# Transfers recorded by modelled readiness on their queue, and the softmax reciprocals broadcast by four short transfers a unit

## The chip, the cores and the metric

One core of one Trainium2 chip. The metric is the device time of one execution in microseconds (us). "Before" is the kernel without the change, "after" the kernel with it.

## The reference

Two layers of attention and a gated feed-forward block, batch 1, 2048 tokens, width 512, 32 heads of 16, feed-forward width 1792, bfloat16 inputs:

```python
x = A_x
for _ in range(2):
    n = layernorm(x)
    q, k, v = heads_of(n @ wqkv)                    # 32 heads of 16
    x = x + (softmax(q @ k.T / 4) @ v) @ wo
    n = layernorm(x)
    x = x + (gelu(n @ w_gate) * (n @ w_up)) @ w_down
```

## The kernel before

The kernel's Python code is itself a scheduler. It keeps a modelled clock for each engine, always picks what can start next, and *records* it. What is recorded is a fixed order of instructions on each engine, with semaphore waits between them. If an engine's next instruction is not ready, the engine stands: in the profile below TensorE stood 16.8 us in all before matmuls whose input had not landed. So the numbers that the scheduler *books* for an instruction or a transfer decide the order, and the chip then executes that order with the durations that the trace shows.

A transfer is booked as 0.5 us of its queue, `kb / 180` us of a shared wire, and 1.7 us to land:

```python
def dma(eng, grp, dst, src, r=(), w=(), serial=False, kb=32):
    ...
    t = max(sch.free[eng], sch.ready(eng, r, w)) + 0.5
    wire[0] = max(t, wire[0]) + kb / 180.0
    return sch.op(eng, lambda e: e.dma_start(dst, src), r=r, w=w, grp=grp, cost=0.5, lat=wire[0] - t + 1.7)
```

A *unit* is four heads for 512 query tokens. After its scores, exponentials and products with V, the unnormalised output lies in `OS` (128 partitions: 32 for each head, of which 16 hold the output, one the sum). A query block has eight units. For each half of them the sums are gathered into `LT`, inverted by VectorE, stored to a scratch tensor in HBM, and broadcast back to the partitions of `OS`; GpSimd (POOL) multiplies. Odd units land in `ATS` and are moved into the other half of `AT` by four small transfers. Then TensorE can do the output projection (`AT` times `WO`), and the feed-forward of this query block runs between the attention of the next ones:

```python
def normalise(layer, qb, gs, half):
    ...                                              # checks, reciprocal of LT on VectorE
    def then(o):
        dma("sp", "rs%d" % half, RSC[half, 0:np_, :], LT[0:np_, :], r=lk, w=[("RSC", half)], serial=True)
        rest = list(enumerate(gs))
        def spread():
            ...                                      # next unit, one of NRB = 2 buffers
            dma("sp", "rb%d" % slot, RB[:, slot, :],
                AP(RSC, (half * 16 * HB + 16 * i) * 128, [[512, 4], [0, 32], [1, 512]]),
                r=[("RSC", half)], w=[("RB", slot)], serial=True, kb=256)
            ...
            def done(o):
                if odd:
                    for j in range(4):
                        dma("sp", "at%d_%d" % (c % 2, j), AT[32 * j + 16:32 * j + 32, c, :],
                            ATS[32 * j:32 * j + 16, c % 2, :], r=[("ATS", c % 2)], w=[("ATo", c, j)], serial=True)
                ...
                spread()
            job("pool", 1, [(lambda e: e.tensor_tensor(dst, OS[:, os_, :], RB[:, slot, :], op=ALU.mult), ...)], done)
        for _ in range(NRB):
            spread()
    dve(1, ops, then)
```

Every transfer that SyncE (SP) issues is recorded at the moment at which the code comes upon it, even if it will only be ready some us later; what is recorded after it on that queue waits behind it. The feed-forward weights come on the same queue, in chunks of 256 KB through six buffers:

```python
def wload():
    ...
    dma("sp", "wr%d" % s, dst, src, w=[("WR", s)], serial=True, kb=256)
```

and `w_down` is read once for each of a query block's four tiles, except at the end of the program, where four accumulators are held at once:

```python
wlist += [("d", i) for _ in range(1 if tail else 4) for i in range(NFT // 2)]
```

Of the kernel before, what the change touches and what calls it, by code (L numbers as in the profile page):

```python
# [11 lines left out]
ALU = mybir.AluOpType  # L12
# [163 lines left out]
def _emit_fast(nc, es, x_in, wqkv, wo, wg, wu, wd, out, n_rep=2):  # L176
# [179 lines left out]
    def late_init():  # L356
        sch.op("pool", lambda e: e.memset(AP(VP, 16, [[NKT * H * VW, 128], [VW, NKT * H]]), 1.0), w=[("VPONE",)])
        sch.op("pool", lambda e: e.memset(OKL[:], 1.0), w=[("OKL",)])
        sch.op("pool", lambda e: e.memset(OKV[:], 1.0), w=[("OKV",)])
        sch.op("pool", lambda e: e.memset(LT[:], 1.0), w=[("LT", i) for i in range(HB)])  # L360
# [6 lines left out]
    for layer in range(n_rep):  # L367
        for qb in range(NQB):
            tail = layer == n_rep - 1 and qb == NQB - 1
            wlist += [("g", i) for i in range(NFT // 2)] + [("u", i) for i in range(NFT // 2)]  # L370
            wlist += [("d", i) for _ in range(1 if tail else 4) for i in range(NFT // 2)]
    wst = {"loaded": 0, "next": 0}

    def wload():
        i = wst["loaded"]
        if i >= len(wlist):
            return
        wst["loaded"] += 1
        kind, k = wlist[i]
        s = i % NWR  # L380
        if kind == "d":
            dst = WR[:, s, 0:2 * D].rearrange("p (a b) -> p a b", a=2)
            src = wd_src[:, 2 * k:2 * k + 2, :]
        else:
            dst = WR[:, s, 0:NCK * 256].rearrange("p (a b) -> p a b", a=NCK)
            src = (wg_src if kind == "g" else wu_src)[:, :, 256 * k:256 * (k + 1)]
        dma("sp", "wr%d" % s, dst, src, w=[("WR", s)], serial=True, kb=256)

    def wget(kind, k):
        i = wst["next"]  # L390
        assert wlist[i] == (kind, k), (wlist[i], kind, k)
        wst["next"] += 1
        while wst["loaded"] < i + NWR:
            if wst["loaded"] >= len(wlist):
                break
            wload()
        return i % NWR


    jobs = {"dve": [], "pool": []}  # L400
    now = [0.0]
# [7 lines left out]
    def dve(prio, ops, then=None, ported=False):  # L409
        job("dve", prio, ops, then, ported)  # L410

    def starts_of(eng):
        out = []
# [5 lines left out]
    def pump_one(t):  # L419
        for eng in ("dve", "pool"):  # L420
            if not jobs[eng] or sch.free[eng] >= t:
# [143 lines left out]

    xloaded = set()

    def xset(n):
        return [4 * (n % 2) + i for i in range(4)]

    def xload(n):
# [6 lines left out]
        if layer:  # L578
            dma("sp", "xl%d" % (n % 2), X[:, sl[0]:sl[0] + 4, :], XS[rows, :].rearrange("(a p) c -> p a c", p=128),
                r=[("XS", 4 * qb + i) for i in range(4)], w=[("X", x) for x in sl], serial=True, kb=1024)  # L580
        else:
            def issue():
                return dma("pool", "xp%d" % (n % 2), X[:, sl[0]:sl[0] + 4, :],
                           x_in[0, rows, :].rearrange("(a p) c -> p a c", p=128),
                           w=[("X", x) for x in sl], serial=True, kb=1024)
            job("pool", 3, [(issue, [], [("X", x) for x in sl], None)])

# [112 lines left out]
    gq = []  # L700
    rb_no = [0]

    def normalise(layer, qb, gs, half):
# [12 lines left out]
        def then(o):  # L716
            dma("sp", "rs%d" % half, RSC[half, 0:np_, :], LT[0:np_, :], r=lk, w=[("RSC", half)], serial=True)
            rest = list(enumerate(gs))

            def spread():  # L720
                if not rest:
                    return
                i, g = rest.pop(0)
                slot = rb_no[0] % NRB
                rb_no[0] += 1
                dma("sp", "rb%d" % slot, RB[:, slot, :],
                    AP(RSC, (half * 16 * HB + 16 * i) * 128, [[512, 4], [0, 32], [1, 512]]),
                    r=[("RSC", half)], w=[("RB", slot)], serial=True, kb=256)
                os_ = os_of.pop((layer, qb * NG + g))
                c, odd = g // 2, g % 2  # L730
                dst = ATS[:, c % 2, :] if odd else AT[:, c, :]
                wk = [("ATS", c % 2)] if odd else [("AT", c)] + [("ATo", c, j) for j in range(4)]

                def done(o):
                    if odd:

                        for j in range(4):
                            dma("sp", "at%d_%d" % (c % 2, j), AT[32 * j + 16:32 * j + 32, c, :],
                                ATS[32 * j:32 * j + 16, c % 2, :], r=[("ATS", c % 2)], w=[("ATo", c, j)], serial=True)
                    os_free.append(os_)  # L740
                    done_n[0] += 1
                    if done_n[0] == n:
                        have.add(("norm", layer, qb, gs[-1]))
                    spread()
                job("pool", 1, [(lambda e: e.tensor_tensor(dst, OS[:, os_, :], RB[:, slot, :], op=ALU.mult),  # L745
                                 [("OS", os_), ("RB", slot)], wk, 1.35)], done)

            for _ in range(NRB):
                spread()
        dve(1, ops, then)  # L750

    def evac(layer, u, part):
# [11 lines left out]
        def then(o):  # L764
# [9 lines left out]
            while g >= lo + sizes[k]:  # L774
                lo += sizes[k]
                k += 1
            i = g - lo
            dma("sp", "lt%d" % i, LT[16 * i:16 * i + 16, :],
                AP(OS, 16 * NOS * 512 + s * 512, [[32 * NOS * 512, 4], [1, 512]]),
                r=[("OS", s)], w=[("LT", i)], serial=True)  # L780
            units_done[layer] += 1
            if i == sizes[k] - 1:
                normalise(layer, qb, list(range(lo, lo + sizes[k])), k % 2)
            if g == NG - 1:
# [25 lines left out]
    def post(layer, qb):  # L810
# [6 lines left out]
        xload(n_)  # L817
        while ("norm", layer, qb, NG - 1) not in have or n_ not in xloaded:
            yield None
# [18 lines left out]
        for k in range(NFT // 2):  # L838
            s = wget("u", k)
            for jj in range(2):  # L840
# [7 lines left out]
        for ts in ([tts] if tail else [[tt] for tt in tts]):  # L848
            bs = None
            for k in range(NFT // 2):  # L850
                s = wget("d", k)

# [15 lines left out]
            for tt, b in zip(ts, bs):  # L868
                i = tt % 4
                x = xsl[i]  # L870
                if last:
                    ob = XNT[:, i % NCK, 512 * qb + (i // NCK) * D:512 * qb + (i // NCK) * D + D]

                    def store(o, i=i, tt=tt, ob=ob):
                        dma("sp", "st%d" % i, out[0, tt * 128:(tt + 1) * 128, :], ob, r=[("OB", i)], serial=True)
                        have.add(("out", tt))
                    evac_job(1, b, [(lambda e, b=b, x=x, ob=ob: e.tensor_tensor(ob, bank(b)[:, 0:D], X[:, x, :],
# [5 lines left out]
                else:  # L883
                    def keep(o, i=i, tt=tt, x=x):
                        dma("sp", "xs%d" % i, XS[tt * 128:(tt + 1) * 128, :], X[:, x, :], r=[("X", x)],
                            w=[("XS", tt)], serial=True, kb=256)
                        stats(i, x, got(("st", (layer, qb, 1), i)))
                        if i == 3:
                            have.add(("xs", layer + 1, qb))
                    evac_job(1, b, [(lambda e, b=b, x=x: e.tensor_tensor(X[:, x, :], bank(b)[:, 0:D], X[:, x, :],  # L890
# [88 lines left out]
    def fill_ready():  # L979
# [6 lines left out]
        if gq:  # L986
            qb, k = gq[0]
            if wst["loaded"] <= wst["next"]:
                return None
# [22 lines left out]
    def g_slot(qb, k):  # L1012
        b0 = slot_banks()[0]
        take_slot()
        xs = slice(512 * qb, 512 * (qb + 1))
        s = wget("g", k)

# [184 lines left out]
    def head_source(b):  # L1202
# [6 lines left out]
        if b:  # L1209
            while b not in xloaded:  # L1210
                yield None
# [991 lines left out]
```

## Time and profile before

| | before |
|---|---|
| median, first three timed runs | 1823.64 us |
| span of the profiled run | 1823.5 us |
| ScalarE busy | 1530.2 us (84%) |
| TensorE busy | 1681.1 us, of which 271.8 are clock-keeping matmuls (zero weights; the scheduler inserts them in a function named `keep_clock`) |
| VectorE busy | 1410.7 us |

The page of the kernel before, its table of costliest groups (line, engine, operation, output and inputs, shapes, count, then busy us and mean ns, then the engine's idle time just before them and what ended most of it):

```profile
L1067 ACT ACTIVATE fPT<-fPS 128x1024 bf16<-128x1024 f32 (+1 forms) x1408 | 1449.9, 1175 | 177.1 <-PE fPS L1062 173.1
L1101 DVE TENSOR_SCALAR fPI<-fPS 128x512 int16<-128x512 f32 x956 | 631.0, 686 | 222.3 <-PE fPS L1062 218.5
...
L1192 PE MATMUL fPS<-fONB,fZV 128*17 128x512 bf16 x3496 | 271.8, 387 | 5.2 <-POOL fONB L344 4.1
```

ScalarE's exponentials (line 1067) set the pace: windows of 20 us without a disturbance show it busy for 20.00 of them. What there is to win is therefore its idle time, 293 us. I sorted every gap of ScalarE into kinds. *Head* is before 75 us, *tail* after the last exponential, *boundary* a gap of over 9 us in between (they lie between the layers), *GELU* a gap before a GELU. A gap is put down to the *projection* or the *weights* where TensorE, at that place or within 6 us before it, stood 0.4 us or more before a matmul that reads `fAT`, or a weight chunk. The rest is *other*.

TensorE's waits in the kernel before (engine, line, waited for: us in total, times, longest us):

```profile
PE fPS L1062 <- ACT fPT L1067: 51.4, 195, 0.6
PE fPS L554 <- DMA fAT<-fATS: 16.8, 7, 3.2
PE fPS L858 <- DMA fWR<-in_B_w_down_dram: 14.1, 10, 5.2
```

The first line is TensorE waiting for the pace setter, which is as it should be. The second and third are not: here TensorE stands before the output projection, or before the down projection, while exponentials could have been fed. The next view, the windows, shows what this costs at one projection (window; us; busy us and count of PE, PEld, DVE, ACT, POOL; granted clock of TensorE; DMA share; GB/s):

```profile
260.00:280.00 20.00, 16.56 (x156) 4.00 (x156) 11.23 (x19) 14.18 (x14) 2.54 (x2) 0.83 0.08 25
```

ScalarE loses 5.8 of these 20 us, and TensorE's clock falls to 0.83. The timeline of SP before shows how this came about (start us, us for the merged stretch, engine, line, operation, output<-input, count):

```profile
248.34 0.51 SPq L276 DMA_DIRECT2D rscr<-fLT  x1
250.16 7.14 SPq L276 DMA_DIRECT2D fRB<-rscr  x3
259.44 2.47 SPq L276 DMA_DIRECT2D fAT<-fATS  x4
261.95 0.58 SPq L276 DMA_DIRECT2D fRB<-rscr  x1
268.50 2.42 SPq L276 DMA_DIRECT2D fAT<-fATS  x4
```

and the timeline of POOL, with its idle time and releaser in brackets, shows when the broadcasts were there:

```profile
255.50 1.27 POOL L745 TENSOR_TENSOR fAT<-fOS,fRB 128x512 bf16<-128x512 f32 x1 [79.01 <-DMA fRB<-rscr]
258.15 1.27 POOL L745 TENSOR_TENSOR fATS<-fOS,fRB 128x512 bf16<-128x512 f32 x1 [1.38 <-DMA fRB<-rscr]
261.70 1.27 POOL L745 TENSOR_TENSOR fAT<-fOS,fRB 128x512 bf16<-128x512 f32 x1 [2.28 <-DMA fRB<-rscr]
267.20 1.27 POOL L745 TENSOR_TENSOR fATS<-fOS,fRB 128x512 bf16<-128x512 f32 x1 [4.23 <-DMA fRB<-rscr]
```

The first product starts 5.3 us after the first broadcast was issued, and the scheduler had booked 0.5 + 256/180 + 1.7 = 3.6 us for that broadcast. The records of the packets say why it is slow: a broadcast is 128 packets of 2 KB with a median of 84 ns, and in these 7 us never more than 6 of them were in flight together. The trace also has the updates of the semaphore that tells of a landing: each of the 64 broadcasts shows one update about 1 us after its issue begins and then four separate ones as its data land, the last of them 5.2 us after the first issue here. So it lands in four parts, as many as its leading dimension has members.

At the layer boundary the same things stand in one chain. The chain of waits before, from where ScalarE stops at 874.55 (start us, us, what):

```profile
872.73 1.81 DMA rscr<-fLT
...
875.17 7.59 DMA fRB<-rscr
...
882.91 1.28 POOL fATS L745
884.19 0.02 issue
884.21 0.58 SPq L276
...
887.35 5.74 DMA fWR<-in_B_w_down_dram
893.09 0.04 issue
893.13 1.03 PE fPS L858 x2
```

The broadcast is late, so POOL is late, so the AT copies that were recorded ahead of the weights are late, and a `w_down` chunk is issued only at 887. Nothing else held it: SP's list of waits in this stretch has no wait for a weight buffer.

### The profile page before, as it was taken

How to read it: one execution, taken by the hardware profiler on the slowest of the kernel's cores; microseconds unless marked ns; L12 is line 12 of the kernel's file. 1: busy time of each engine (PE TensorE's matmuls, PEld its weight loads, DVE VectorE, ACT ScalarE, POOL GpSimd, SP SyncE). 2: the span in 40 equal slices, each digit the busy share in tenths (PEclk: the TensorE clock that was granted, in tenths of full speed). 3: DMA queues.
4: the chain of work that ended last, by engine and by line, in shares of the span. 5: the costliest groups of instructions: out<-in, count | busy, mean ns of one | idle time of the engine just before them, and what ended most of it. 6: DMA issues, size and time to landing. Idle time of an engine off the chain costs nothing.

```text
span 1823.5 us, 39987 instructions
## 1 busy us (share of the span) xinstructions
PE 1681.1 (92%) x17053; PEld 512.5 (28%) x17053; DVE 1410.7 (77%) x2322; ACT 1530.2 (84%) x1484; POOL 216.4 (12%) x237
## 2 busy tenths in 40 slices
PE   8998989999898998999899989899989999899998
PEld 3422223222232222322332322232223222232233
DVE  4798876889868878699568598769876988768853
ACT  2699998989889998899289389889998999889931
POOL 2402010011111021010331120101010010101010
PEclk9999999999999999999999999999999999999999
DMA  5200000152022410223312500023501152023403
GB/s 151 71 2 29 2 28 26 53 156 80 28 65 80 145 54 11 58 81 99 109 47 70 168 28 3 28 60 89 158 28 36 48 163 62 28 61 110 127 21 100
DMA packets 142775, 126.14 MB, mean 69 GB/s; under 512 B 8704, under 2 KB 126208, under 8 KB 142592
## 3 DMA queue, kind: packets, MB, share of 16 engines
q1 hardware_dynamic: 138320, 115.12, 21.1%
q0 software_dynamic: 4272, 8.39, 1.7%
q8 instruction: 139, 2.28, 0.5%
q14 instruction: 44, 0.36, 0.1%
HBM read 109.84 MB, written 6.82 MB: 64 GB/s over the span
## 4 chain that ended last, share of the span: by engine, by line
ACT 38%; PE 34%; DVE 12%; DMA 11%; SPq 2%; POOL 2%; issue 1%; POOLq 0%; DVEq 0%
ACT fPT L1067 37%; PE fPS L1062 7%; PE fPS L1172 7%; PE fPS L554 7%; PE fPS L1021 5%; DMA fRB<-rscr 5%; DVE fPI L1101 4%; PE fPS L1192 4%; DVE fPP L1123 3%; PE fPS L858 3%; DMA fWR<-in_B_w_down_dram 3%; SPq L276 2%; POOL fATS L745 1%; DVE fQ L596 1%; DMA rscr<-fLT 1%
## 5 line engine op out<-in xcount | busy, mean ns | idle before, releaser
L1067 ACT ACTIVATE fPT<-fPS 128x1024 bf16<-128x1024 f32 (+1 forms) x1408 | 1449.9, 1175 | 177.1 <-PE fPS L1062 173.1
L1101 DVE TENSOR_SCALAR fPI<-fPS 128x512 int16<-128x512 f32 x956 | 631.0, 686 | 222.3 <-PE fPS L1062 218.5
L1062 PE MATMUL fPS<-fQ,fKT 32*128 32x512 bf16 x4096 | 545.1, 388 | 69.4 <-ACT fPT L1067 51.4
L1123 DVE TENSOR_SCALAR fPP<-fPI 128x2048 int16<-128x2048 int16 x717 | 490.3, 722 | 7.1 <-PE fPS L1172 4.7
L1172 PE MATMUL fPS<-fPT,fVP 128*17 128x512 bf16 x3140 | 441.8, 387 | 8.7 <-DVE fOS L761 2.7
L1172 PE MATMUL fPS<-fPP,fVD 128*17 128x512 f16 x2868 | 374.9, 387 | 10.9 <-DVE fPP L1123 9.5
L1062 PEld LDWEIGHTS fPS<-fQ,fKT 32*128 32x128 bf16 x4096 | 136.5, 91 | 603.0 <-ACT fPT L1067 494.7
L1192 PE MATMUL fPS<-fONB,fZV 128*17 128x512 bf16 x3496 | 271.8, 387 | 5.2 <-POOL fONB L344 4.1
L1172 PE MATMUL fPS<-fPI,fVP 128*17 128x512 f16 x956 | 267.6, 388 | 2.5 <-DVE fPP L1123 2.5
L745 POOL TENSOR_TENSOR fAT<-fOS,fRB 128x512 bf16<-128x512 f32 x32 | 43.6, 1362 | 922.4 <-DMA fRB<-rscr 922.4
L1172 PEld LDWEIGHTS fPS<-fPT,fVP 128*17 128x17 f16 x3140 | 100.6, 88 | 159.5 <-issue 104.7
L858 PE MATMUL fPS<-fWR,fHT 128*128 128x512 bf16 x448 | 126.7, 386 | 14.4 <-DMA fWR<-in_B_w_down_dram 14.1
L1172 PEld LDWEIGHTS fPS<-fPP,fVD 128*17 128x17 f16 x2868 | 89.5, 89 | 121.6 <-issue 50.5
L554 PE MATMUL fPS<-fXNT,fWR 128*128 128x512 bf16 x448 | 113.9, 382 | 1.9 <-DVE fHT L844 1.5
L1027 ACT ACTIVATE fHT<-fPS 128x1024 bf16<-128x1024 f32 x56 | 57.3, 1023 | 69.5 <-PE fPS L1021 69.4
L844 DVE TENSOR_TENSOR fHT<-fPS,fHT 128x512 bf16<-128x512 f32 x112 | 76.8, 688 | 49.8 <-PE fPS L554 49.3
L1192 PEld LDWEIGHTS fPS<-fONB,fZV 128*17 128x17 f16 x3496 | 80.4, 91 | 80.7 <-issue 38.0
L1021 PE MATMUL fPS<-fXNT,fWR 128*128 128x512 bf16 x448 | 99.3, 380 | 0.9 <-ACT fPT L1067 0.7
L1172 PEld LDWEIGHTS fPS<-fPI,fVP 128*17 128x17 f16 x956 | 58.4, 88 | 49.6 <-issue 30.0
L629 POOL TENSOR_SCALAR fVD<-fVP 128x544 f16<-128x544 f16 (+1 forms) x48 | 53.2, 1110 | 154.1 <-DVE fVP L637 151.4
L1021 PEld LDWEIGHTS fPS<-fXNT,fWR 128*128 128x128 bf16 x448 | 42.6, 98 | 55.2 <-issue 3.1
L745 POOL TENSOR_TENSOR fATS<-fOS,fRB 128x512 bf16<-128x512 f32 x32 | 44.1, 1378 | 106.0 <-DMA fRB<-rscr 106.0
(58 smaller groups left out, 705.8 us busy)
## 6 DMA issues: line engine op xcount, KB each, us to landing
fWR<-in_B_w_down_dram SPq DMA_DIRECT2D x203, 256.0 KB, 3.2
fRB<-rscr SPq DMA_DIRECT2D x64, 256.0 KB
fWR<-in_B_w_gate_dram SPq DMA_DIRECT2D x56, 256.0 KB, 3.3
fWR<-in_B_w_up_dram SPq DMA_DIRECT2D x56, 256.0 KB, 2.9
fX<-in_A_x_dram POOLq DMA_DIRECT2D x7, 1024.0 KB, 5.7
xscr<-fX SPq DMA_DIRECT2D x16, 256.0 KB, 2.3
fX<-xscr SPq DMA_DIRECT2D x4, 1024.0 KB, 5.8
fAT<-fATS SPq DMA_DIRECT2D x128, 16.0 KB, 1.8
```

The source lines that it names most:

```text
L554: ins = e.matmul(bank(bs[0])[:, 0:cols], lhsT=l, rhs=r_, start=(i == 0), stop=(i == n - 1))
L745: job("pool", 1, [(lambda e: e.tensor_tensor(dst, OS[:, os_, :], RB[:, slot, :], op=ALU.mult), [("OS", os_), ("RB", slot)], wk, 1.35)], done)
L844: (lambda e: e.tensor_tensor(HT[:, ft, :], bank(b), HT[:, ft, :], op=ALU.mult), [BK[b], ("HT", ft)], [("HT", ft)], 0.62)], got(("up", laye ...
L858: ins = e.matmul(bank(b)[:, 0:D], lhsT=HT[:, ft, i * 128:(i + 1) * 128], rhs=WR[:, s, jj * D:(jj + 1) * D], start=(ft == 0), stop=(ft == N ...
L1021: ins = e.matmul(bank(b0 + jj), lhsT=wchunk(s, jj, ck), rhs=XNT[:, ck, xs], start=(ck == 0), stop=(ck == NCK - 1))
L1027: sch.op("act", lambda e: e.activation(HT[:, 2 * k:2 * k + 2, :], PS[:, b0:b0 + 2, :], ACTF.Gelu_apprx_tanh), r=bks, w=[("HT", 2 * k), ("H ...
L1062: ins = e.matmul(bank(b0 + k), lhsT=KT[32 * j:32 * j + 32, c, kt * 128:(kt + 1) * 128], rhs=Q[32 * j:32 * j + 32, qs, :], start=True, stop ...
L1067: o = sch.op("act", lambda e: e.activation(PT[:, p, 0:512 * na].rearrange("p (a b) -> p a b", a=na), PS[:, b0:b0 + na, :], ACTF.Exp, scale ...
L1101: dve(0, [(lambda e: e.tensor_scalar(PI[:, gi, 512 * r:512 * (r + 1)], bank(b0 + n - 1), DBIAS, 0.0, op0=ALU.add, op1=ALU.max), [bks[-1]], ...
L1123: shifts.append((s, [(lambda e: e.tensor_scalar(PP[:, s, :], PI[:, gi, :], int(OCT) * ph // NPH, None, op0=ALU.add), [("PI", gi, r) for r ...
L1172: ins = e.matmul(PS[32 * j:32 * j + VW, ACC, :], lhsT=l, rhs=r_, start=a, stop=z, tile_position=(0, 32 * j), skip_group_check=True)
L1192: ins = e.matmul(PS[32 * j:32 * j + VW, ACC, :], lhsT=ZV[:, :], rhs=ones, start=False, stop=False, tile_position=(0, 32 * j), skip_group_c ...
```

## The change

The intent is twofold. Transfers on SP become jobs, as VectorE's and POOL's work already was: they are recorded when the modelled clock says that they are ready and the queue is free, by priority (short transfers of the normalisation 0, weights 1, loads and stores of X 2). And the broadcast becomes four transfers a unit, each writing only the 16 partitions of a head that hold output, with the 16 copies as the leading dimension. The rows between are cleared once. The short transfers are booked at `dma`'s default of 32 KB, so the fourth of a unit is booked to land 4 x 0.5 + 32/180 + 1.7 = 3.9 us after the first issue begins.

```diff
+        sch.op("pool", lambda e: e.memset(RB[:], 0.0), w=[("RB", i, j) for i in range(NRB) for j in range(4)])
...
-        dma("sp", "wr%d" % s, dst, src, w=[("WR", s)], serial=True, kb=256)
+        keys = [("WR", s)]
+        job("sp", 1, [(lambda: dma("sp", "wr%d" % s, dst, src, w=keys, serial=True, kb=256), [], keys, None)],
+            lambda o: wst["here"].add(i))
...
-    jobs = {"dve": [], "pool": []}
+    jobs = {"dve": [], "pool": [], "sp": []}
...
+    def move(prio, grp, dst, src, r, w, then=None, kb=32):
+
+        job("sp", prio, [(lambda: dma("sp", grp, dst, src, r=r, w=w, serial=True, kb=kb), r, w, None)], then)
...
-        for eng in ("dve", "pool"):
+        for eng in ("dve", "pool", "sp"):
...
-                dma("sp", "rb%d" % slot, RB[:, slot, :],
-                    AP(RSC, (half * 16 * HB + 16 * i) * 128, [[512, 4], [0, 32], [1, 512]]),
-                    r=[("RSC", half)], w=[("RB", slot)], serial=True, kb=256)
...
+            for j in range(4):
+                move(0, "rb%d_%d" % (slot, j), RB[32 * j:32 * j + 16, slot, :],
+                     AP(RSC, (half * 16 * HB + 16 * i + 4 * j) * 128, [[0, 16], [1, 512]]),
+                     [("RSC", half)], [("RB", slot, j)], landed)
```

Cut here: the loads and stores of X, the gather of the sums, the copies of AT and the stores of the output go through `move` in the same way; pieces of the feed-forward wait until their chunk has been recorded; the gather of the next half waits until the last half has left `LT`.

More of the change, by code (lines that the diff above doesn't have):

```diff
@@ L371, in _emit_fast @@
             wlist += [("d", i) for _ in range(1 if tail else 4) for i in range(NFT // 2)]
-    wst = {"loaded": 0, "next": 0}
+    wst = {"loaded": 0, "next": 0, "here": set()}
     def wload():
@@ L396, in wget, with wneed @@
             wload()
+        return i
+    def wneed(kind, k):
+        i = wget(kind, k)
+        while i not in wst["here"]:
+            yield None
         return i % NWR
-    jobs = {"dve": [], "pool": []}
+    jobs = {"dve": [], "pool": [], "sp": []}
     now = [0.0]
@@ L566, in _emit_fast @@
     xloaded = set()
+    xhere = {0}
     def xset(n):
@@ L578, in xload @@
         if layer:
-            dma("sp", "xl%d" % (n % 2), X[:, sl[0]:sl[0] + 4, :], XS[rows, :].rearrange("(a p) c -> p a c", p=128),
-                r=[("XS", 4 * qb + i) for i in range(4)], w=[("X", x) for x in sl], serial=True, kb=1024)
+            move(2, "xl%d" % (n % 2), X[:, sl[0]:sl[0] + 4, :], XS[rows, :].rearrange("(a p) c -> p a c", p=128),
+                 [("XS", 4 * qb + i) for i in range(4)], [("X", x) for x in sl], lambda o: xhere.add(n), kb=1024)
         else:
@@ L585, in issue @@
                            w=[("X", x) for x in sl], serial=True, kb=1024)
-            job("pool", 3, [(issue, [], [("X", x) for x in sl], None)])
+            job("pool", 3, [(issue, [], [("X", x) for x in sl], None)], lambda o: xhere.add(n))
     def qproj(layer, up):
@@ L701, in _emit_fast @@
     rb_no = [0]
+    lt = {"held": False, "next": []}
     def normalise(layer, qb, gs, half):
@@ L716, in then @@
         def then(o):
-            dma("sp", "rs%d" % half, RSC[half, 0:np_, :], LT[0:np_, :], r=lk, w=[("RSC", half)], serial=True)
-            rest = list(enumerate(gs))
-            def spread():
-                if not rest:
-                    return
-                i, g = rest.pop(0)
-                slot = rb_no[0] % NRB
-                rb_no[0] += 1
-                dma("sp", "rb%d" % slot, RB[:, slot, :],
-                    AP(RSC, (half * 16 * HB + 16 * i) * 128, [[512, 4], [0, 32], [1, 512]]),
-                    r=[("RSC", half)], w=[("RB", slot)], serial=True, kb=256)
-                os_ = os_of.pop((layer, qb * NG + g))
-                c, odd = g // 2, g % 2
-                dst = ATS[:, c % 2, :] if odd else AT[:, c, :]
-                wk = [("ATS", c % 2)] if odd else [("AT", c)] + [("ATo", c, j) for j in range(4)]
-                def done(o):
-                    if odd:
-                        for j in range(4):
-                            dma("sp", "at%d_%d" % (c % 2, j), AT[32 * j + 16:32 * j + 32, c, :],
-                                ATS[32 * j:32 * j + 16, c % 2, :], r=[("ATS", c % 2)], w=[("ATo", c, j)], serial=True)
-                    os_free.append(os_)
-                    done_n[0] += 1
-                    if done_n[0] == n:
-                        have.add(("norm", layer, qb, gs[-1]))
-                    spread()
-                job("pool", 1, [(lambda e: e.tensor_tensor(dst, OS[:, os_, :], RB[:, slot, :], op=ALU.mult),
-                                 [("OS", os_), ("RB", slot)], wk, 1.35)], done)
@@ L748, in then, with stored, count, spread @@
-            for _ in range(NRB):
+            move(0, "rs%d" % half, RSC[half, 0:np_, :], LT[0:np_, :], lk, [("RSC", half)], stored)
+        def stored(o):
+            lt["held"] = False
+            while lt["next"]:
+                lt["next"].pop(0)()
+            for _ in range(NRB):
+                spread()
+        rest = list(enumerate(gs))
+        def count():
+            done_n[0] += 1
+            if done_n[0] == n:
+                have.add(("norm", layer, qb, gs[-1]))
+        def spread():
+            if not rest:
+                return
+            i, g = rest.pop(0)
+            slot = rb_no[0] % NRB
+            rb_no[0] += 1
+            here = []
+            def landed(o):
+                here.append(o)
+                if len(here) == 4:
+                    job("pool", 1, [(lambda e: e.tensor_tensor(dst, OS[:, os_, :], RB[:, slot, :], op=ALU.mult),
+                                     [("OS", os_)] + [("RB", slot, j) for j in range(4)], wk, 1.35)], done)
+            for j in range(4):
+                move(0, "rb%d_%d" % (slot, j), RB[32 * j:32 * j + 16, slot, :],
+                     AP(RSC, (half * 16 * HB + 16 * i + 4 * j) * 128, [[0, 16], [1, 512]]),
+                     [("RSC", half)], [("RB", slot, j)], landed)
+            os_ = os_of.pop((layer, qb * NG + g))
+            c, odd = g // 2, g % 2
+            dst = ATS[:, c % 2, :] if odd else AT[:, c, :]
+            wk = [("ATS", c % 2)] if odd else [("AT", c)] + [("ATo", c, j) for j in range(4)]
+            def done(o):
+                os_free.append(os_)
+                if not odd:
+                    count()
+                    spread()
+                    return
+                moved = []
+                def put(o):
+                    moved.append(o)
+                    if len(moved) == 4:
+                        count()
+                for j in range(4):
+                    move(0, "at%d_%d" % (c % 2, j), AT[32 * j + 16:32 * j + 32, c, :],
+                         ATS[32 * j:32 * j + 16, c % 2, :], [("ATS", c % 2)], [("ATo", c, j)], put)
@@ L777, in then, with gathered, gather @@
             i = g - lo
-            dma("sp", "lt%d" % i, LT[16 * i:16 * i + 16, :],
-                AP(OS, 16 * NOS * 512 + s * 512, [[32 * NOS * 512, 4], [1, 512]]),
-                r=[("OS", s)], w=[("LT", i)], serial=True)
             units_done[layer] += 1
-            if i == sizes[k] - 1:
-                normalise(layer, qb, list(range(lo, lo + sizes[k])), k % 2)
+            def gathered(o):
+                if i == sizes[k] - 1:
+                    lt["held"] = True
+                    normalise(layer, qb, list(range(lo, lo + sizes[k])), k % 2)
+            def gather():
+                move(0, "lt%d" % i, LT[16 * i:16 * i + 16, :],
+                     AP(OS, 16 * NOS * 512 + s * 512, [[32 * NOS * 512, 4], [1, 512]]),
+                     [("OS", s)], [("LT", i)], gathered)
+            if lt["held"]:
+                lt["next"].append(gather)
+            else:
+                gather()
             if g == NG - 1:
@@ L817, in post @@
         xload(n_)
-        while ("norm", layer, qb, NG - 1) not in have or n_ not in xloaded:
+        while ("norm", layer, qb, NG - 1) not in have or n_ not in xhere:
             yield None
@@ L838, in post @@
         for k in range(NFT // 2):
-            s = wget("u", k)
+            s = yield from wneed("u", k)
             for jj in range(2):
@@ L850, in post @@
             for k in range(NFT // 2):
-                s = wget("d", k)
+                s = yield from wneed("d", k)
                 def fn(e, bs, s=s, k=k, ts=ts):
@@ L874, in store @@
                     def store(o, i=i, tt=tt, ob=ob):
-                        dma("sp", "st%d" % i, out[0, tt * 128:(tt + 1) * 128, :], ob, r=[("OB", i)], serial=True)
-                        have.add(("out", tt))
+                        move(2, "st%d" % i, out[0, tt * 128:(tt + 1) * 128, :], ob, [("OB", i)], [], got(("out", tt)), kb=128)
                     evac_job(1, b, [(lambda e, b=b, x=x, ob=ob: e.tensor_tensor(ob, bank(b)[:, 0:D], X[:, x, :],
@@ L884, in keep @@
                     def keep(o, i=i, tt=tt, x=x):
-                        dma("sp", "xs%d" % i, XS[tt * 128:(tt + 1) * 128, :], X[:, x, :], r=[("X", x)],
-                            w=[("XS", tt)], serial=True, kb=256)
+                        move(2, "xs%d" % i, XS[tt * 128:(tt + 1) * 128, :], X[:, x, :], [("X", x)], [("XS", tt)],
+                             got(("xs", layer + 1, qb)) if i == 3 else None, kb=256)
                         stats(i, x, got(("st", (layer, qb, 1), i)))
-                        if i == 3:
-                            have.add(("xs", layer + 1, qb))
                     evac_job(1, b, [(lambda e, b=b, x=x: e.tensor_tensor(X[:, x, :], bank(b)[:, 0:D], X[:, x, :],
@@ L987, in fill_ready @@
             qb, k = gq[0]
-            if wst["loaded"] <= wst["next"]:
+            if wst["next"] not in wst["here"]:
                 return None
@@ L1015, in g_slot @@
         xs = slice(512 * qb, 512 * (qb + 1))
-        s = wget("g", k)
+        s = wget("g", k) % NWR
         def fn(e):
@@ L1209, in head_source @@
         if b:
-            while b not in xloaded:
+            while b not in xhere:
                 yield None
```

## The prediction

> **What bounds the kernel now.** The page: span 1823.5 us, ScalarE busy 1530 us (84%), TensorE 1681 us, of which 272 are clock-keeping matmuls (line 1192), VectorE 77%. In 20 us windows ScalarE is busy 19 to 20 us through most of attention: the exponentials of line 1067 set the pace (37% of the chain of waits). To win is ScalarE's 293 us of idleness. Its gaps in the timeline: head 51 us; GELU phases about 32; layer boundary 32.3 (at 874) and 28.6 (at 1017); tail 33 before and some 30 after the last GELUs; six groups of 4.4 to 6.0 us (270, 484, 689, 1161, 1366, 1571), together 32, where TensorE waits 2.2 to 3.2 us for fAT<-fATS before the output projection; and about 14 us (382, 591, 804, 1281, 1675) where it waits for w_down chunks, as it also does for 5.2 us inside the gap at 874.
>
> **Why.** TensorE's order is fixed by the scheduler in the kernel, which books a reciprocal broadcast at about 3.6 us. The chain of waits shows 6.8 to 7.6 us for the first pair, 5.0 to 5.3 later. One broadcast is 128 packets of 2 KB, median 84 ns, with only 4 to 7 in flight. The Trainium skill, "DMA: Bandwidth & Descriptors", section "Rules for kernel authors", says that an outermost dimension under 16 confines a DMA to that many engines; the source here leads with 4. 32 packets x 84 ns is 2.7 us on each of four engines, plus 1.8 us to land; two broadcasts share the four. And as SP's queue is in order, AT copies and broadcasts waiting for POOL hold the weight loads: at 374 to 378 three w_down loads stood behind an AT copy and a broadcast, and TensorE lost 3.1 us at 381. SP waited 175 us for POOL's products.
>
> **What changes.** 64 broadcasts of 256 KB become 256 of 32 KB on up to 16 engines. 192 more issues at about 0.5 us are 100 us of SP time, on a queue mostly idle. Estimated: four issues 2.1 us + 1.8 us landing = 4 us for a unit, 6 for a pair's second, instead of about 7.2 for both. From the second half's first broadcast to the projection was 21.6 us (250.8 to 272.4); I estimate 16 to 18. More important: the booking then fits the chip, and blocked DMAs no longer hold weights. An RB memset on POOL costs a few us off the path. Arithmetic on TensorE, ScalarE and VectorE is unchanged.
>
> **On the critical path.** Recoverable: 32 us of projection waits, 14 of weight waits, 5 to 10 at the first boundary, 3 in the tail: 55 to 60 us. GELU, head and the weight-paced boundary at 1017 stay. I expect some 80%, as the new order brings its own small waits, and faster attention leaves less cover at the boundary.
>
> **Prediction.** 1775 us (-2.7%), range 1748 to 1806. Faster by over 2%: 0.70; within 2%: 0.28; slower: 0.02.
>
> **Right if:** TensorE's waits before the projection drop below about 1 us; w_down waits mostly vanish; RB packets run up to 16 at once; POOL products start about 4 us after the first issue; granted clock after the projections returns from 0.83-0.91 to near 1; ScalarE's busy time stays, its idle falls by about 50 us.
> **Wrong if:** 16 issues a half-block on SP delay the weights; the order drifts elsewhere; the gaps at 874 and 1017 grow by what attention saves; or projection waits persist because another booked time is also short.

## The result, and the profile after

After took 1775.93 us (median of 4 runs, 1773.34 to 1780.14), before 1822.8 us (4 runs). The ratio is 0.9742, 95% interval 0.9716 to 0.9767. Ratios here are the mean time of one kernel's fast runs over that of the other's in the same rounds, so not quite the ratio of the medians; in the ratios of the experiments further down the first, profiled execution of each kernel is left out.

| ScalarE, us of the profiled run | before | after | difference |
|---|---|---|---|
| span | 1823.5 | 1771.6 | -51.9 |
| busy | 1530.2 | 1522.0 | -8.2 |
| gaps: projection | 30.6 | 0.5 | -30.1 |
| gaps: weights | 9.9 | 0.1 | -9.8 |
| gaps: layer boundary (first + second) | 32.3 + 28.6 | 13.2 + 41.9 | -5.8 |
| gaps: head | 52.2 | 50.0 | -2.2 |
| gaps: GELU | 32.4 | 30.9 | -1.5 |
| gaps: tail | 65.4 | 64.8 | -0.6 |
| gaps: other | 42.0 | 48.1 | +6.1 |

The page after, the groups that answer to those shown:

```profile
L1112 ACT ACTIVATE fPT<-fPS 128x1024 bf16<-128x1024 f32 (+1 forms) x1408 | 1441.8, 1170 | 134.5 <-PE fPS L1107 133.0
L1146 DVE TENSOR_SCALAR fPI<-fPS 128x512 int16<-128x512 f32 x968 | 637.3, 683 | 172.7 <-PE fPS L1107 170.8
...
L1237 PE MATMUL fPS<-fONB,fZV 128*17 128x512 bf16 x3296 | 259.8, 387 | 5.3 <-POOL fONB L344 4.1
```

Most of the 8 us of ScalarE's busy time follow from VectorE's line: the scheduler gave it 12 more tiles of the exponential (968 instead of 956). On ScalarE 12 exponentials of 1536 columns (1503 ns each before) became ones of 1024 (1077 ns), which is some 5 us. Why the scheduler chose so was not followed.

TensorE's waits after. Both DMA lines are gone from the list of the matmuls' waits altogether (its weight loads still wait 0.8 us in all for `w_down`):

```profile
PE fPS L1107 <- ACT fPT L1112: 58.2, 218, 0.9
PE fPS L567 <- issue: 11.1, 70, 0.2
PE fPS L1217 <- DVE fPP L1168: 8.5, 17, 0.9
```

The same window after: ScalarE 19.73 of 20 us, clock 1.00.

```profile
260.00:280.00 20.00, 18.87 (x212) 5.28 (x206) 17.34 (x29) 19.73 (x20) 1.28 (x1) 1.00 0.05 11
```

SP's timeline after:

```profile
247.19 0.51 SPq L276 DMA_DIRECT2D rscr<-fLT  x1
249.01 6.27 SPq L276 DMA_DIRECT2D fRB<-rscr  x12
256.24 2.47 SPq L276 DMA_DIRECT2D fAT<-fATS  x4
258.75 1.97 SPq L276 DMA_DIRECT2D fRB<-rscr  x4
263.56 2.41 SPq L276 DMA_DIRECT2D fAT<-fATS  x4
```

POOL's timeline after:

```profile
252.28 1.28 POOL L759 TENSOR_TENSOR fAT<-fOS,fRB 128x512 bf16<-128x512 f32 x1 [81.37 <-DMA fRB<-rscr]
254.94 1.27 POOL L759 TENSOR_TENSOR fATS<-fOS,fRB 128x512 bf16<-128x512 f32 x1 [1.38 <-DMA fRB<-rscr]
256.87 1.27 POOL L759 TENSOR_TENSOR fAT<-fOS,fRB 128x512 bf16<-128x512 f32 x1 [0.66 <-DMA fRB<-rscr]
262.26 1.28 POOL L759 TENSOR_TENSOR fATS<-fOS,fRB 128x512 bf16<-128x512 f32 x1 [4.12 <-DMA fRB<-rscr]
```

The first product starts 3.3 us after the first issue instead of 5.3, the fourth 13.3 us instead of 17.0, and now up to 16 packets of 2 KB are in flight at once. The semaphore of each of the 256 short transfers shows sixteen updates where the long one had four. And yet the output projection itself did not come sooner. TensorE's first matmul on `fWO` stands at 271.8 us after, at 272.4 before. Counted from the first issue of the half, it came 22.8 us later in after and 22.2 us later in before. The copies of AT, whose last issue ended at 266.0, had several us to spare. So this chain was not shortened where it ends; it was made to agree with the place at which TensorE had been told to expect it. Whether that agreement is the cause is what the experiments ask.

The boundary, seen by ScalarE's timeline, before and then after (the last figure in brackets is the gap):

```profile
906.86 5.71 ACT L1067 ACTIVATE fPT<-fPS 128x1536 bf16<-128x1536 f32 x5 [32.31 <-PE fPS L1062]
...
1045.57 4.69 ACT L1067 ACTIVATE fPT<-fPS 128x1024 bf16<-128x1024 f32 x5 [28.62 <-PE fPS L1062]
```

```profile
866.04 5.54 ACT L1112 ACTIVATE fPT<-fPS 128x1536 bf16<-128x1536 f32 x5 [13.17 <-PE fPS L1107]
...
1017.51 2.85 ACT L1112 ACTIVATE fPT<-fPS 128x1024 bf16<-128x1024 f32 x3 [41.91 <-PE fPS L1107]
```

At the first gap ScalarE runs out 21.7 us earlier and resumes 40.8 us earlier. At the second it runs out 41.3 us earlier but resumes only 28.1 us earlier: some of what attention had gained was given back. The last experiment shows that the 28 chunks of `w_down` that pass in this gap set a part of it.

### The profile page after: what moved, and what is told of

Its sections match the earlier page's. It is cut to its first block, busy times and chain, and to the rows that moved or that the text cites. A ratio compares the mean times of both kernels' runs of the same rounds, so it can differ in the third digit from the quotient of the medians.

```text
span 1771.6 us, 39808 instructions
## 1 busy us (share of the span) xinstructions
PE 1628.3 (92%) x16712; PEld 509.2 (29%) x16889; DVE 1415.4 (80%) x2343; ACT 1522.0 (86%) x1484; POOL 218.7 (12%) x238
## 3 DMA queue, kind: packets, MB, share of 16 engines
q1 hardware_dynamic: 138064, 106.74, 20.8%
## 4 chain that ended last, share of the span: by engine, by line
ACT 50%; PE 34%; DVE 14%; issue 1%; POOL 1%; DMA 1%; DVEq 0%; POOLq 0%
ACT fPT L1112 49%; PE fPS L1107 7%; PE fPS L1217 7%; PE fPS L1066 5%; DVE fPI L1146 5%; PE fPS L567 5%; PE fPS L1237 5%; DVE fPP L1168 4%; PE fPS L906 4%; DVE fHT L892 1%; DVE fQ L610 1%; PE fPS L630 1%; ACT L1112 1%; DMA fX<-in_A_x_dram 0%; POOL fVD L643 0%
## 5 line engine op out<-in xcount | busy, mean ns | idle before, releaser
L1217 PE MATMUL fPS<-fPP,fVD 128*17 128x512 f16 x2904 | 384.3, 383 | 6.8 <-DVE fPP L1168 5.5
L1237 PE MATMUL fPS<-fONB,fZV 128*17 128x512 bf16 x3296 | 259.8, 387 | 5.3 <-POOL fONB L344 4.1
L1217 PEld LDWEIGHTS fPS<-fPP,fVD 128*17 128x17 f16 x2904 | 92.4, 88 | 114.2 <-issue 51.9
L906 PE MATMUL fPS<-fWR,fHT 128*128 128x512 bf16 x397 | 115.4, 382 | 8.7 <-issue 6.7
L1072 ACT ACTIVATE fHT<-fPS 128x1024 bf16<-128x1024 f32 x56 | 57.3, 1024 | 67.3 <-PE fPS L1066 67.2
L567 PE MATMUL fPS<-fXNT,fWR 128*128 128x512 bf16 x397 | 104.6, 381 | 9.6 <-issue 5.1
L1066 PE MATMUL fPS<-fXNT,fWR 128*128 128x512 bf16 x432 | 97.1, 379 | 2.4 <-ACT fPT L1112 1.2
L1237 PEld LDWEIGHTS fPS<-fONB,fZV 128*17 128x17 f16 x3296 | 75.3, 91 | 76.4 <-issue 37.5
L525 POOL TENSOR_SCALAR fLNS<-fMV 128x4 f32<-128x4 f32 x16 | 5.8, 361 | 469.0 <-DVE fMV L518 469.0
```

The costliest lines, as they stand in the source:

```text
L567: ins = e.matmul(bank(bs[0])[:, 0:cols], lhsT=l, rhs=r_, start=(i == 0), stop=(i == n - 1))
L906: ins = e.matmul(bank(b)[:, 0:D], lhsT=HT[:, ft, i * 128:(i + 1) * 128], rhs=WR[:, s, jj * D:(jj + 1) * D], start=(ft == 0), stop=(ft == N ...
L1066: ins = e.matmul(bank(b0 + jj), lhsT=wchunk(s, jj, ck), rhs=XNT[:, ck, xs], start=(ck == 0), stop=(ck == NCK - 1))
L1072: sch.op("act", lambda e: e.activation(HT[:, 2 * k:2 * k + 2, :], PS[:, b0:b0 + 2, :], ACTF.Gelu_apprx_tanh), r=bks, w=[("HT", 2 * k), ("H ...
L1217: ins = e.matmul(PS[32 * j:32 * j + VW, ACC, :], lhsT=l, rhs=r_, start=a, stop=z, tile_position=(0, 32 * j), skip_group_check=True)
L1237: ins = e.matmul(PS[32 * j:32 * j + VW, ACC, :], lhsT=ZV[:, :], rhs=ones, start=False, stop=False, tile_position=(0, 32 * j), skip_group_c ...
```

## The experiments

Two parts of the change can be told apart: the short broadcast (with its booking), and the recording by readiness. Theory B says that the gain comes from the late broadcast; the rival O says that it comes from the order on SP's queue. Within B it is open whether the transfer's speed or its booking counts. All kernels gave correct results; each was timed in three rounds with the kernel before on the same chip. They were run in three groups on three chips, on which the kernel before took 1825.42 us (the first four), 1823.19 us (32 rows, weights at once, the control, the better version) and 1827.71 us (bookings of 40 and 48 KB after that); between groups the ratios compare better than the us.

### The short broadcasts alone

```diff
-                dma("sp", "rb%d" % slot, RB[:, slot, :],
-                    AP(RSC, ..., [[512, 4], [0, 32], [1, 512]]), r=[("RSC", half)], w=[("RB", slot)], serial=True, kb=256)
+                for j in range(4):
+                    dma("sp", "rb%d_%d" % (slot, j), RB[32 * j:32 * j + 16, slot, :],
+                        AP(RSC, ... + 4 * j ..., [[0, 16], [1, 512]]), r=[("RSC", half)], w=[("RB", slot, j)], serial=True)
```

Cut here: `RB` is cleared once, and POOL's product waits for the four parts.

> The kernel before with the four short broadcasts alone; transfers are recorded at once, as before. Theory B (the late broadcast, through TensorE's waits before the output projection, is most of the gain): these waits of 2.2 to 3.2 us fall below 1 us, ScalarE's gaps of 4 to 6 us there go, and the time is about 1790 us (-33), the weight waits shrinking too because the queue is held less long. Rival O (the order on SP's queue is most of the gain): 1805 us or more, w_down waits of 1 to 5 us still there.

Measured: 1785.55 us, ratio 0.9787 (0.9764 to 0.9810). Gaps for the projection 0.0 us, for the weights 0.1 us, and no wait of TensorE for AT or a weight chunk in its list. So both kinds of waits go with the broadcast alone, though nothing was done for the weights. This is what B expected, and it is some 39 us (0.0213 of before) of the 47 that the whole change gave (0.0258).

### The recording by readiness alone

```diff
-            for j in range(4):
-                move(0, "rb%d_%d" % (slot, j), RB[32 * j:32 * j + 16, slot, :], ..., landed)
+            move(0, "rb%d" % slot, RB[:, slot, :], AP(RSC, ..., [[512, 4], [0, 32], [1, 512]]),
+                 [("RSC", half)], [("RB", slot, j) for j in range(4)], landed, kb=256)
```

Cut here: POOL's product waits for the one part instead of four.

> The kernel after with one 256 KB broadcast a unit, led by a dimension of 4 and booked as before; all else recorded by readiness. Theory B: the projection waits of 2 to 3 us stay (broadcasts still 5 to 7 us), about 1805 us (-18), the gain coming from the weights and the first layer boundary. Rival O: 1790 us or less, with short projection waits.

Measured: 1807.43 us, ratio 0.9902 (0.9880 to 0.9925). TensorE's waits in this run:

```profile
PE fPS L567 <- DMA fAT<-fATS: 18.8, 7, 3.6
PE fPS L905 <- DMA fWR<-in_B_w_down_dram: 2.5, 2, 1.3
```

The projection waits stay (gaps of 27.3 us), and those for the weights fall from 14.1 to 2.5 us; 18 us are won. So recording by readiness does keep weights from standing behind other transfers; but once the broadcast is on time there is nothing left for it to prevent. Not all of the 18 us is of the weights: ScalarE was also busy 9.5 us less (1520.7 us), with 16 more tiles on VectorE, and the control below shows that the order alone can move the time by as much.

### The booking alone

One number of the kernel before is changed; the transfer is the slow one.

```diff
-                    r=[("RSC", half)], w=[("RB", slot)], serial=True, kb=256)
+                    r=[("RSC", half)], w=[("RB", slot)], serial=True, kb=470)
```

> The kernel before with one number changed: the scheduler books a broadcast at 470 KB instead of 256, so that it lands at about 4.8 us, a pair's second at 7.4, as the trace shows. The transfer itself is as before. If it is the wrong booking that costs (TensorE is sent to wait where it could have worked): projection waits vanish, about 1795 us (-28). If it is the length of the chain through the broadcast: 1815 us or more.

Measured: 1789.97 us, ratio 0.9807 (0.9782 to 0.9832). Nothing in this program is quicker: in all eight halves before a projection the first product starts 5.1 to 6.0 us after the first issue (before 4.9 to 5.6). SP and POOL at the example, in this run:

```profile
251.58 7.00 SPq L276 DMA_DIRECT2D fRB<-rscr  x3
...
256.78 1.27 POOL L745 TENSOR_TENSOR fAT<-fOS,fRB 128x512 bf16<-128x512 f32 x1 [80.78 <-DVE fPI L1101]
```

The profile names VectorE as what ended POOL's wait here, but the broadcast's last semaphore update came at 256.64, 0.14 us before the product.

But the projection comes later (24.6 to 26.9 us after the first issue in seven of the eight blocks, where before had 21.8 to 22.7 us in six of them), other work stands in its place, and the waits are all but gone:

```profile
PE fPS L858 <- DMA fWR<-in_B_w_down_dram: 4.6, 4, 2.5
...
PE fPS L554 <- DMA fAT<-fATS: 1.6, 2, 1.0
```

A correct number in the scheduler gave some 35 us (0.0193 of before) of the 47 that the whole change gave (0.0258), on a transfer as slow as ever. For the projection and weight waits it is the booking that costs. The total is less sure: one booking was tried, and the control below shows how far a total moves with the order alone.

### Readiness with the slow broadcast, booked correctly

The edit is that of the second experiment, with `kb=470` in place of `kb=256`.

> Order by readiness, one slow 256 KB broadcast, booked at 470 KB (its true length). If the booking is what counts and not the broadcast's speed: within 10 us of the kernel after (about 1780). If the speed counts: 1795 us or more.

Measured: 1800.89 us (1793.74 to 1804.96, a wide spread), ratio 0.9875. The expectation for the booking was missed: the total is not within 10 us of after, and by what was put down beforehand (1795 us or more) it speaks for the speed. Yet projection gaps are 0.0 us and weight gaps 1.0 us, so the booking did its work where it was aimed. What is longer are mainly the boundary gaps, 69.5 us where after has 55.1, which is 14 of the 20 us between the two profiled runs. Whether the slow broadcast lengthens them or the order does, no run separates; the control below moves the boundary by 8 us with the transfer unchanged. So the total was a poor thing to set the expectation on, and that speed counts at the boundary is not ruled out.

### Sixteen engines or half the bytes

```diff
-                move(0, "rb%d_%d" % (slot, j), RB[32 * j:32 * j + 16, slot, :],
-                     AP(RSC, ..., [[0, 16], [1, 512]]),
+                move(0, "rb%d_%d" % (slot, j), RB[32 * j:32 * j + 32, slot, :],
+                     AP(RSC, ..., [[0, 32], [1, 512]]),
```

> The kernel after with each short broadcast writing 32 rows instead of 16: 64 KB each, so the 256 KB a unit of before, but still led by a multiple of 16. If the number of engines is what made the broadcast quick: landing stays at 1.8 to 2.0 us, up to 16 packets in flight, time within 5 us of the kernel after (1776). If the bytes did it: landing at 3 us or more and a time of 1790 or more.

Measured: 1773.11 us, ratio 0.9721 (0.9705 to 0.9738). With the bytes of before the median from issue to landing is 2.0 us where after has 1.8; the issues of after and then of this run:

```profile
fRB<-rscr SPq DMA_DIRECT2D x256, 32.0 KB, 1.8
fRB<-rscr SPq DMA_DIRECT2D x256, 64.0 KB, 2.0
```

The first product starts 3.4 to 4.2 us after the first issue (after 3.3 to 4.5), up to 14 packets are in flight at the example, and the time is the same. The recorded order of every engine equals that of after. So the halved bytes do next to nothing. Two things still differ from before, the leading dimension and the number of transfers, and no run changes one without the other. The trace tells them apart: each transfer of this run lands in sixteen parts by itself, as each of after does, and the broadcast led by four landed in four. At the example the two units issued first moved their 256 packets in 4.4 us here and in 5.9 us before.

### The weights recorded at once again

```diff
-        job("sp", 1, [(lambda: dma("sp", "wr%d" % s, dst, src, w=keys, serial=True, kb=256), [], keys, None)],
-            lambda o: wst["here"].add(i))
+        dma("sp", "wr%d" % s, dst, src, w=keys, serial=True, kb=256)
+        wst["here"].add(i)
```

> The kernel after with one part undone: weight chunks are recorded at once again (in the order of asking), all else by readiness. If holding the weights behind other transfers was a cost of its own: w_down waits of 1 us and more come back and the time is 1785 to 1800. If the short broadcast had already removed the cause of the holding: within 6 us of 1776.

Measured: 1781.83 us, ratio 0.9781 (0.9764 to 0.9797). Weight gaps 0.1 us; no matmul waits for `w_down`, and its weight loads wait 1.1 us in all. The time is 5.9 us above that of after, just inside the 6 us put down. The weights need no order of their own once the broadcast is short.

### A control: the same program with another booking

Up to here differences of 5 to 10 us tempt one to explain them. This run changes nothing that the chip executes except the order that follows from 0.09 us more for each short broadcast.

```diff
-                     [("RSC", half)], [("RB", slot, j)], landed)
+                     [("RSC", half)], [("RB", slot, j)], landed, kb=48)
```

> A control for the scatter of the static order: the kernel after with each short broadcast booked at 48 KB instead of 32 (0.09 us more each); nothing runs differently but the recorded order. Expected within 8 us of 1776; a larger difference would mean that differences of that size between the other runs say nothing.

Measured: 1793.74 us, ratio 0.9846 (0.9829 to 0.9864). That is 18 us slower than after, where I had expected at most 8. Its projection and weight gaps are as small as in after (0.6 and 0.1 us); the boundary has 62.7 us instead of 55.1 and "other" 59.7 instead of 48.1, which with small rises elsewhere is the whole difference. By what was put down before the run, differences of this size between single kernels say nothing of their parts.

### Three pairs, to tell readiness from scatter

So the split alone and the whole change were both run at three bookings of the short broadcast (one edit of `kb` each).

> Short broadcasts with transfers recorded at once, booked at 40 KB each instead of 32: with the two next runs and those already made, three pairs (32, 40, 48 KB) of the split alone against the whole change. If recording by readiness is worth something of its own, the whole change is ahead in all three pairs, by about 10 us. If what differs is the scatter of the order, the pairs disagree in sign: split alone at 40 KB anywhere from 1775 to 1800 us.

> As the run before, booked at 48 KB; the whole change took 1794 us at this booking. Readiness is worth something: about 1804 us. Scatter alone: anywhere from 1775 to 1800 us. In either case projection and weight waits stay near zero, as the broadcast is short.

> The whole change with the short broadcasts booked at 40 KB: between 1770 and 1796 us if the scatter of the order is what the control at 48 KB showed; projection and weight waits near zero.

| booked KB | split alone, us (ratio) | whole change, us (ratio) |
|---|---|---|
| 32 | 1785.55 (0.9787) | 1775.93 (0.9742) |
| 40 | 1780.06 (0.9746) | 1794.83 (0.9822) |
| 48 | 1779.66 (0.9735) | 1793.74 (0.9846) |

The pairs disagree in sign. In none of these six kernels do the projection and weight gaps come to more than 0.7 us together. So a gain from recording by readiness *beside* the short broadcast is not shown; if anything the split alone did better on average (ratios 0.9756 against 0.9803). With three bookings, and only the pair at 40 KB known to be from one chip, this is no proof that it does harm.

### An attempt at a better version

The second boundary gap of after (41.9 us) lies in a stretch in which 28 chunks of `w_down` pass, four times the same seven: its first down-projection matmul starts at 971.8 us, its last ends at 1006.9, so a chunk takes some 1.25 us (the 1.4 quoted below was taken from part of it). With attention out of work there, the banks for four accumulators can be borrowed, as the end of the program does.

```diff
-            wlist += [("d", i) for _ in range(1 if tail else 4) for i in range(NFT // 2)]
+            wlist += [("d", i) for _ in range(1 if qb == NQB - 1 else 4) for i in range(NFT // 2)]
...
-        for ts in ([tts] if tail else [[tt] for tt in tts]):
+        for ts in ([tts] if qb == NQB - 1 else [[tt] for tt in tts]):
```

> An attempt at a better version: the kernel after, where the last query block of layer 0 reads w_down once for its four tiles (four banks held), as the last block of layer 1 does, instead of once for each tile. ScalarE's gap at 976 (41.9 us, in which 28 chunks pass at about 1.4 us each) should shrink by 12 to 20 us: 1756 to 1764. If the gap is set by the layer norm and the projections of the next layer and not by the weights: within 5 us of 1776.

Measured: 1762.69 us (1760.64 to 1763.45), ratio 0.9666 (0.9650 to 0.9683), the fastest kernel. The second gap in ScalarE's timeline:

```profile
1006.02 4.77 ACT L1112 ACTIVATE fPT<-fPS 128x1024 bf16<-128x1024 f32 x5 [28.65 <-PE fPS L1107]
```

It is 13.3 us shorter than in after, and the kernel's median is 13.2 us lower. Since the control warned of luck, it was tried again at the booking that had been slow:

> The better version (w_down read once at the last block of layer 0) at the booking of 48 KB, where the kernel after took 1794 us. If its gain of 13 us is of the gap at the layer boundary and not luck of the order: about 1780 us (-10 to -18), the second boundary gap near 28 us instead of 38.

Measured: 1785.27 us, ratio 0.9769 (0.9747 to 0.9791), against 0.9846 for the same booking without it. The second gap in this run, and in the control at the same booking without the edit:

```profile
1021.73 8.44 ACT L1112 ACTIVATE fPT<-fPS 128x1024 bf16<-128x1024 f32 x9 [28.44 <-PE fPS L1107]
...
1027.71 7.53 ACT L1112 ACTIVATE fPT<-fPS 128x1024 bf16<-128x1024 f32 x8 [37.89 <-PE fPS L1107]
```

By the ratios a gain of about 0.8% (some 14 us) shows at both bookings. At the first all of it lies in the gap at which it was aimed; at the second that gap accounts for 9.5 us, and the rest is within what the order scatters.

## Why the prediction was right

Point by point:

- **Projection waits.** Predicted to give back 32 us; 30.1 us came back, TensorE's waits for AT went from 16.8 us to none, and the granted clock in the window returned from 0.83 to 1.00. Right.
- **Their cause.** "The booking then fits the chip" was called the more important part. The booking-alone run shows it directly for the projection waits, which went from 16.8 us to 1.6 with the transfer unchanged; the time fell by some 35 us. Right.
- **Sixteen packets at once, product about 4 us after the first issue.** At most 16 against 6 at the example, and 3.3 to 4.5 us over the eight blocks. The Trainium skill's page "DMA: Bandwidth & Descriptors", section "Rules for kernel authors", was the ground for this, and the 32-row run, with full bytes on a leading dimension of 32, agrees with it. The semaphores agree too: four parts landed for each broadcast of before, sixteen for each short one.
- **"I estimate 16 to 18" us from the first broadcast to the projection.** Wrong: 22.8 us, against 22.2 before. I had taken the chain to end in the projection. It ends in an order fixed beforehand: the data were ready earlier (last AT issue ended 17.0 us after the first broadcast, not 20.8), and TensorE came when it was told to. The error cost nothing that the gaps show (0.5 us before the projections in all): the gain was in what TensorE did meanwhile.
- **Weight waits, 14 us.** By the sorting used here they were 9.9 us of gaps, and 9.8 came back. Right that they go, somewhat less in size; and of the two reasons given, the booking and the recording, each is nearly enough by itself: recording alone took the waits from 14.1 to 2.5 us, the split alone took all of them. They don't add up.
- **Boundaries.** Predicted: 5 to 10 us at the first, nothing at the second. Measured: 19.1 us shorter and 13.3 us longer. The warning that the gaps might "grow by what attention saves" came true at the second, so the sum (-5.8 us) fell where expected by two errors of opposite sign. That is luck.
- **Tail.** 3 us expected, 0.6 us measured.
- **ScalarE's busy time stays.** It fell by 8.2 us, some 5 of them because VectorE was given 12 more tiles. This was not foreseen. The idle time fell by 43.8 us, not by about 50.

The sum came out within 1 us of the measurement; that precision is luck. The controls put the same change with a slightly different booking at 1794 and 1795 us, which would have been within the stated range but near its slow end. What is well shown is the removal of 35 to 40 us of projection and weight gaps in every version with a short or correctly booked broadcast; the remaining 10 us either way hang on the boundary gaps and the small gaps of the order that happens to come out.

Left open: which decision of the scheduler turns 0.09 us of booking into a boundary gap 8 us longer was not followed to its start. And whether a faster broadcast is worth anything where it is booked correctly is not settled: of the two runs with the slow, correctly booked one, 1790 us lies within the range of the six with the short one (1776 to 1795 us), and 1801 us lies above it.

## What to carry to other kernels

Where an instruction order is fixed ahead by a model, first compare what the model books for a transfer with what the trace shows: a booking that was too short (3.6 us, where the landing took 5.2) sent TensorE to stand 2.2 to 3.2 us before six of the eight projections, and correcting the number was here worth most of what speeding up the transfer was. Before explaining a difference of 1% between two such schedules, run the same program with a booking moved by a trifle and see how far the time moves by itself; then judge parts by the gaps at which they were aimed, not by the total. And look at the leading dimension of a small broadcast's access pattern: four members gave a first product after about 5 us, sixteen one after 3.3 to 4.5 us, and twice the bytes on a leading dimension of 32 changed that little (3.4 to 4.2 us).

## What the Trainium skill lacked or had wrong

- "DMA: Bandwidth & Descriptors", "Rules for kernel authors", advises to coalesce many small transfers into one large one, since "under 64 KB you're paying mostly overhead". Here the four transfers of 32 KB beat one of 256 KB (first product 3.3 to 4.5 us after the first issue instead of 4.9 to 5.6 us), and the semaphore updates put that down to the large one's leading dimension of 4 (it landed in four parts, each short one in sixteen). The page's own rule on using all 16 engines decides, and the advice on coalescing does not mention it.
- That page's "Latency and other measured facts" has first-byte times but no duration for one issue on SP's queue; elsewhere the page has only a count of sequencer cycles for "previous generations", in its passage on another chip. The runs show a median of 561 ns for the three-dimensional broadcast and 420 ns for each short one (302 ns at least), and four short issues hold the queue for 1.7 us at least and 1.8 us in the median.
- None of the pages consulted on DMA and on traces says that in a statically ordered kernel a transfer's *booked* length can matter more than its real one: some 35 us of 1823 from a single number, and 18 us of scatter from 0.09 us a transfer.
